# Chunked attention before two feed-forward layers: a block's scores taken one group earlier, beside the transposes of the block before it

## The chip, the core and the metric

The kernel runs on one core of a Trainium2 chip. The metric is the device time of one execution in microseconds (us). Five engines of the core matter here: TensorE (PE in the profile, with its weight loads as PEld), VectorE (DVE), ScalarE (ACT), GpSimd (POOL), and SyncE (SP), which issues the transfers. Each engine takes its instructions in the order in which the program lists them; when the instruction at the head waits, everything behind it on that engine waits too.

## What is computed

Attention over chunks of 64 positions feeds a layer with a cosine gate, and that feeds a second layer without one (4608 tokens, width 512, hidden sizes 2048 and 1024; all in float32):

```python
scores = scale * np.matmul(q_c, k_c.transpose(0, 1, 2, 4, 3))
scores = scores - np.max(scores, axis=-1, keepdims=True)
attn = np.exp(scores)
attn = attn / (np.sum(attn, axis=-1, keepdims=True) + 1e-09)
out = np.matmul(attn, v_c)
...
h = x @ w_in
g = h * np.cos(h)
x = g @ w_out
...
a = x @ w1
b = x @ w2
h = a * b @ w3
return h @ w_out
```

## The kernel before

The 4608 tokens are 9 tiles of 512, numbered 0 to 8. Attention works on 36 blocks of 128 tokens, four to a tile. Every float32 product of the layers is made of three matmuls (lines L107 to L109) on operands that are split into a high and a low half.

The first pass runs over the tiles, and in each tile over five groups of 256 hidden columns of the first layer. While tile n is multiplied, the four blocks of tile n+1 go through attention: block j in one of the first four groups. The fifth group, the end group, has no block; there the finished tile n+1 (`xf`) is split into the seven operands `X` of the next tile (`x_op`, L103: high half on ACT, low half on DVE). Tiles 2 to 7 are of this form. In tile 8 no block is left. A second pass and the second layer follow; there is no attention in them.

What stands where on each engine is written out by hand, as a string with one letter for each step. For the groups of tiles 2 to 8 these are `ORDER1` and, for the end group, `ORDER1E`:

- `1`, `2`, `5`, `3`: the hidden product by seven half-size products of six matmuls each (one in `1`, two in each other step). The results go to PSUM tiles `ps_hh`, which share two banks (pool `ps_h`). DVE adds them: `2` ends with the add `d` (L509), `5` with `e` (L519) and `d` (L521), `3` with `e` (L528). Step `3` needs the bank that the add `d` of step `2` frees.
- `a` `c`, `A` `C`, `b` `d`, `B` `D`: the cosine gate on the halves `d` and `e`: L567 on ACT, L572 on DVE, the cosine L577 on ACT, the product L581 on DVE.
- `s`: the gated group of the step before is split, high half on ACT (L589), low half on POOL (L590), two of each. `x` and `y`: the two halves of the output product of that group, 12 matmuls each into four accumulators `acc`.
- `l`, `m`, `h`, `r`: one weight of a later stage is rebuilt from bit halves (L254 and L289 on ACT; L264 to L267 and L295 on DVE) and written to DRAM. For every second `w_in` weight, `m` also forms sums (L281 to L284). `M`, `H`, `R`: such sums for the weights of groups 0 to 4, the last two of them in tile 2.
- `q`: the next step of the block's attention, in the order scores (L377 on PE; then on DVE the maximum, L386, and the subtraction, L388), exponential (L394 on ACT), sum, reciprocal and scaling (L399 to L402 on DVE, L403 on POOL), transposes (L410 on PE, L413 on ACT), values (L424 on PE, L429 on ACT). Scores, transposes and values share the two banks of the pool `ps_at`.

In an order string the five `q` of a group thus stand for a whole block: the scores behind step `2`, exponential and scaling behind step `5`, the transposes behind `x`, the values behind `y`.

Of the kernel before, what the change touches and what calls it, by code (L numbers as in the profile page):

```python
# [9 lines left out]
F32 = mybir.dt.float32  # L10
# [7 lines left out]
P = 128  # L18
# [3 lines left out]
NJ = NT // P  # L22
HP = 4
CC = 4
G1 = 8
GA = 5
# [11 lines left out]
ORDER0 = "PsvaAqQvqcCqxybBdvDqvq"  # L38
ORDER0E = "PsvaAQvcCxybBodDoooL"
ORDER1P = "PsqMhQqqHaclAxqbCrRmBdyqDL"  # L40
ORDER1PE = "SPsQacATCoobBoxodoDyoo"
ORDER1 = "1s2qMh5qqHa3clAxqbCrRmBdyqDL"
ORDER1E = "S1s25a3cATCoobBoxodoDyoo"
ORDER2 = "1s2h5a3clAxbCrdByDm"
ORDER3 = "12sqhlrmq5a3cAbCdBDxy"
ORDER3B = "12sqhrq5a3clAbCmdBDxy"
# [11 lines left out]
def chunk_attention_two_ffn(  # L58
# [20 lines left out]
    ps_h = ctx.enter_context(tc.tile_pool(name="ps_h", bufs=2, space=bass.MemoryType.PSUM))  # L79
    ps_at = ctx.enter_context(tc.tile_pool(name="ps_at", bufs=2, space=bass.MemoryType.PSUM))  # L80
# [128 lines left out]
    def sum_load(g):  # L209
        pair = ("in", g)  # L210
        loaded.append((g, pair, new_w((pair, 2))))
        nc.sync.dma_start(out=f32(W[pair, 2]), in_=wr[g])
# [35 lines left out]
    def st_low():  # L248

        if sat[1] < sat[0]:  # L250
            now["low"] = key = sq[sat[1]]
            sat[1] += 1
            lo = raws[key][:, :, 0]
            nc.scalar.activation(lo.bitcast(I32), lo, AF.Copy, scale=2.0 ** -29)  # L254
# [32 lines left out]
    def st_hi():  # L287
        for _, x, hi, lo in now.get("parts", ()):
            nc.scalar.activation(hi.bitcast(F32R), x, AF.Copy)  # L289
# [72 lines left out]

    def banks_of(j, early, name):
        return [(ps_acc.tile([P, HP, P], F32, tag=f"acc{2 * (j % 2) + c}", name=f"{name}{c}") if early and name == "ps_s"
                 else ps_h.tile([P, HP, P], F32, tag="h", name=f"{name}{c}") if early
                 else ps_at.tile([P, HP, P], F32, tag="at", name=f"{name}{c}"))[:, 0:2].rearrange("p a (b k) -> p (a b) k", k=64)
                for c in range(2)]
# [35 lines left out]

    def att_transpose(j, early):
        ex = att[j]
        ps = ps_at.tile([P, 512], F32, tag="at", name="ps_at")
        for h in range(HP):
            nc.tensor.transpose(ps[:, P * h:P * h + P], ex[:, 2 * h:2 * h + 2].rearrange("p e k -> p (e k)"), ident)  # L410
        pt = (ex.rearrange("p (h c) k -> p h (c k)", c=2) if early
              else wk.tile([P, HP, P], F32, tag="ex", name="pt"))
        nc.scalar.activation(pt, ps.rearrange("p (h t) -> p h t", h=HP), AF.Copy)  # L413
        att[j] = pt
# [18 lines left out]
    def att_tok(step, early):  # L433
        (att_scores, att_softmax, att_scale, att_transpose, att_values)["ABECD".index(step[0])](int(step[1:]), early)
# [144 lines left out]
    def chain_g(i, h, which):  # L579
        t = rr[i, which]  # L580
        nc.vector.tensor_tensor(out=t, in0=t, in1=h, op=ALU.mult)  # L581

    def split_g(i):

        gg[i] = t = one.tile([P, 8, 256], F32R, tag="g", name="g")
        for which in range(2):
            r = rr.pop((i, which)).rearrange("p (i t) -> p i t", i=2)
            hi, lo = (t[:, 2 * s + which:2 * s + which + (6, 4)[which]:(5, 3)[which]] for s in range(2))
            nc.scalar.activation(hi, r, AF.Copy)  # L589
            nc.gpsimd.tensor_tensor(out=lo, in0=r, in1=f32(hi), op=ALU.subtract)  # L590
# [184 lines left out]
    with tc.manual_schedule():  # L775
# [22 lines left out]
        def order_of(i, nth, end):  # L798
            if i < GA:
                return ORDER0E if end else ORDER0  # L800
            if i < 2 * GA:
                return ORDER1PE if end else ORDER1P
            if i <= iA:
                return ORDER1E if end else ORDER1
            if i < iB:
                return ORDER2
            return (ORDER3X if nxt in xs else ORDER3E) if end else ORDER3B if nth else ORDER3
# [3 lines left out]
        iA, iB = (NTILE - 1) * GA, NTILE * GA  # L811
        n_sums = 0
        fq = 0
        for i in range(NG):
            if i == GA:
                sq.extend(("wo2", j) for j in range(FB2))
# [15 lines left out]
            ps, n, g = groups[i]  # L832
            k_tile = (i - iB) // (G1 - GA)
            nxt = PASS2[k_tile + 1] if 0 <= k_tile < NTILE - 1 else None
            nth = (g, g - GA)[ps]
# [14 lines left out]
            for op in order_of(i, nth, end):  # L850
                if op == "s" and i:
                    split_g(i - 1)
                elif op == "x" and i:
                    x2_mm(i - 1, 0)
                elif op == "y" and i:
                    x2_mm(i - 1, 1)
                elif op == "v":
                    conv_tick()
                elif op == "L":
                    if n_sums < GA:  # L860
                        sum_load(n_sums)
                        n_sums += 1
                elif op == "M":
                    if loaded and i > GA + loaded[0][0]:
                        sum_make()
                elif op in "HR":
                    if sp:
                        {"H": sum_hi, "R": sum_lo}[op]()
                elif op == "l":
                    st_low()  # L870
                elif op == "m":
                    st_bits()
                elif op == "h":
                    st_hi()
                elif op == "r":
                    st_lo()
                elif op in "1253PQ":
                    getattr(z, "step" + op)()
                elif op in "ac":
                    chain_t(i, z.d if op == "a" else z.e, "ac".index(op))  # L880
                elif op in "AC":
                    chain_r(i, z.d if op == "A" else z.e, "AC".index(op))
                elif op in "bd":
                    chain_cos(i, "bd".index(op))
                elif op in "BD":
                    chain_g(i, z.d if op == "B" else z.e, "BD".index(op))
                elif op == "q":
                    if i < iA and nth < 4:
                        att_tok(steps[20 * n + 5 * nth + n_q], False)
                    elif i >= iB + FOLD and fq < 4 * FB2:  # L890
                        need(("w3", fq // 2), *(("wo2", j) for j in range(FB2)))
                        fold(fq // 4, fq % 4)
                        fq += 1
                        if fq == 4 * FB2:
                            load_wf(0)
                            load_wf(1)
                    n_q += 1
                elif op in "ST":
                    x_sums("ST".index(op))
                elif op == "o":  # L900
                    if i < GA and not n_o:
                        x_plain()
                    x_op((z.done if i < GA or i >= 2 * GA else OPS)[n_o], n + 1 if ps == 0 else None)
                    n_o += 1
# [62 lines left out]
        j = FB2  # L967
# [75 lines left out]
```

## Time and profile before

| | |
|---|---|
| device time, median of 3 runs | 1493.02 us (1492.53 to 1494.84) |
| the profiled execution | 1494.28 us |
| its span, first to last instruction | 1492.5 us |
| PE busy | 1445.1 us, 97% of the span |
| DVE busy | 1095.9 us, 73% |
| ACT busy | 686.9 us, 46% |
| POOL busy | 265.0 us, 18% |
| mean granted clock of TensorE | 0.992 |

The ends of matmuls are modelled in the profile, so matmuls overlap in it and a busy PE is not the same as a PE that loses nothing. What a wait costs is better read from the distance of starts. The shares are means over stages with different limits.

### The profile page before, as it was taken

The numbers are of one execution on the slowest core, as the hardware profiler recorded it, in microseconds if no ns is written. First come the engines' busy times: TensorE is split into PE (matmuls) and PEld (weight loads), VectorE is DVE, ScalarE is ACT, GpSimd is POOL, SyncE is SP. The second block draws the span as 40 slices with busy tenths as digits, with TensorE's granted clock in tenths as the row PEclk, the third lists the DMA queues.
The fourth block names the chain that finished last, engine by engine and source line by source line (L and its number), as shares of the span: only waits on it lengthen the run. The fifth ranks groups of instructions, "written<-read, shape, count | busy, mean of one in ns | idle before, by whom it ended". The sixth has DMA issues, their size and how long they took to land.

```text
span 1492.5 us, 26013 instructions
## 1 busy us (share of the span) xinstructions
PE 1445.1 (97%) x9996; PEld 1247.4 (84%) x9996; DVE 1095.9 (73%) x1844; ACT 686.9 (46%) x1173; POOL 265.0 (18%) x194
## 2 busy tenths in 40 slices
PE   5789999999999999999999999999999999999998
PEld 4678888888888889988888889998888888888886
DVE  7976788899898886777777777686565666656553
ACT  4767677787777774444444444231031122014002
POOL 0222222223232222211122222122000100200000
PEclk8999999999999999999999999999999999999999
DMA  8654556465664718999889683586435443631501
GB/s 270 198 189 150 211 177 221 155 248 197 219 227 129 247 65 309 369 323 321 306 296 343 240 309 139 203 319 247 150 111 202 159 148 120 224 136 70 212 23 57
DMA packets 122812, 307.38 MB, mean 206 GB/s; under 512 B 13632, under 2 KB 25664, under 8 KB 121536
## 3 DMA queue, kind: packets, MB, share of 16 engines
q1 hardware_dynamic: 122688, 305.71, 58.6%
q8 instruction: 79, 1.29, 0.4%
q14 instruction: 45, 0.37, 0.1%
HBM read 210.50 MB, written 95.16 MB: 205 GB/s over the span
## 4 chain that ended last, share of the span: by engine, by line
PE 73%; DVE 13%; DMA 5%; ACT 5%; issue 2%; POOL 1%; SPq 1%; DVEq 0%; ACTq 0%; POOLq 0%
PE acc L107 10%; PE acc L108 10%; PE acc L109 10%; PE ps_hh L107 9%; PE ps_hh L109 9%; PE ps_hh L108 9%; PE ps_aa L107 5%; PE ps_aa L108 5%; PE ps_aa L109 5%; ACT L394 2%; POOL ex L403 1%; DVE ex L388 1%; DVE t L572 1%; DVE sm L399 1%; DMA sd<-raw 1%
## 5 line engine op out<-in xcount | busy, mean ns | idle before, releaser
L590 POOL TENSOR_TENSOR g<-t,g 128x512 fp32r<-128x512 f32 x144 | 199.1, 1404 | 562.7 <-ACT g L589 512.2
L107 PE MATMUL acc<-g,w 128*128 128x512 f32 x576 | 228.0, 396 | 0.0
L108 PE MATMUL acc<-g,w 128*128 128x512 f32 x576 | 225.5, 392 | 0.0
L109 PE MATMUL acc<-g,w 128*128 128x512 f32 x576 | 224.4, 390 | 0.0
L109 PE MATMUL ps_hh<-T,w 128*128 128x256 f32 (+1 forms) x616 | 182.3, 296 | 6.7 <-DVE w L200 6.6
L107 PE MATMUL ps_hh<-T,w 128*128 128x256 f32 (+1 forms) x616 | 185.1, 300 | 0.0
L108 PE MATMUL ps_hh<-T,w 128*128 128x256 f32 (+1 forms) x616 | 181.8, 295 | 0.0
L109 PEld LDWEIGHTS acc<-g,w 128*128 128x128 f32 x576 | 108.3, 188 | 23.4
L109 PEld LDWEIGHTS ps_hh<-T,w 128*128 128x128 f32 x616 | 118.7, 193 | 10.0 <-DVE w L200 7.5
L108 PEld LDWEIGHTS acc<-g,w 128*128 128x128 f32 x576 | 108.7, 189 | 19.7 <-POOL g L590 0.6
L107 PEld LDWEIGHTS acc<-g,w 128*128 128x128 f32 x576 | 108.6, 189 | 19.7
L107 PE MATMUL ps_hh<-B,w 128*128 128x256 f32 (+1 forms) x396 | 120.2, 304 | 4.2 <-DVE t L581 2.9
L107 PEld LDWEIGHTS ps_hh<-T,w 128*128 128x128 f32 x616 | 118.6, 193 | 5.4
L108 PEld LDWEIGHTS ps_hh<-T,w 128*128 128x128 f32 x616 | 118.6, 193 | 3.2
L108 PE MATMUL ps_hh<-B,w 128*128 128x256 f32 (+1 forms) x396 | 116.4, 294 | 0.0
L109 PE MATMUL ps_hh<-B,w 128*128 128x256 f32 (+1 forms) x396 | 116.2, 294 | 0.0
L764 ACT ACTIVATE phl<-e 128x512 fp32r<-128x512 f32 x32 | 20.2, 633 | 201.9 <-DVE e L762 201.9
L107 PE MATMUL acc<-wf,phl 128*128 128x512 f32 x252 | 98.3, 390 | 1.4 <-DVE o L707 1.4
L577 ACT ACTIVATE t<-t,half_pi 128x512 f32<-128x512 f32 x144 | 98.3, 715 | 1.4
L108 PE MATMUL acc<-wf,phl 128*128 128x512 f32 x252 | 98.1, 389 | 0.0
L109 PE MATMUL acc<-wf,phl 128*128 128x512 f32 x252 | 98.0, 389 | 0.0
L567 ACT ACTIVATE t<-d 128x512 int32<-128x512 f32 x62 | 38.9, 627 | 120.6 <-DVE d L521 117.9
(209 smaller groups left out, 3419.7 us busy)
## 6 DMA issues: line engine op xcount, KB each, us to landing
w<-sd SPq DMA_DIRECT2D x159, 512.0 KB, 5.9
sd<-raw SPq DMA_DIRECT2D x104, 256.0 KB, 4.6
s<-sd SPq DMA_DIRECT2D x43, 256.0 KB, 4.5
qk<-in_q_dram SPq DMA_DIRECT2D x36, 256.0 KB, 4.5
qk<-in_k_dram SPq DMA_DIRECT2D x36, 256.0 KB, 4.6
x2a<-x2o SPq DMA_DIRECT2D x36, 256.0 KB, 3.0
x2a<-x2a SPq DMA_DIRECT2D x36, 256.0 KB, 6.4
x2d<-x2a SPq DMA_DIRECT2D x36, 256.0 KB, 3.1
```

The source lines that it names most:

```text
L107: nc.tensor.matmul(ps, a[0], b[0], start=first, stop=False)
L108: nc.tensor.matmul(ps, a[0], b[1], start=False, stop=False)
L109: nc.tensor.matmul(ps, a[1], b[0], start=False, stop=last)
L388: nc.vector.tensor_tensor(out=ex[:, :, c], in0=ps[c], op=ALU.subtract, in1=mx[:, :, c].unsqueeze(2).to_broadcast([P, HP, 64]))
L394: nc.scalar.activation(ex, ex, AF.Exp, scale=SCALE)
L399: nc.vector.reduce_sum(out=sm, in_=ex, axis=AX.X)
L403: (nc.vector if early else nc.gpsimd).tensor_tensor(out=ex, in0=ex, in1=rc.unsqueeze(2).to_broadcast([P, 2 * HP, 64]), op=ALU.mult)
L567: nc.scalar.activation(t.bitcast(I32), h, AF.Copy, scale=INV2PI, bias=0.25)
L572: nc.vector.scalar_tensor_tensor(t, h, INV2PI, t.bitcast(I32), op0=ALU.mult, op1=ALU.subtract)
L577: nc.scalar.activation(t, t, AF.Sin, scale=TWO_PI, bias=half_pi)
L590: nc.gpsimd.tensor_tensor(out=lo, in0=r, in1=f32(hi), op=ALU.subtract)
L764: nc.scalar.activation(t[:, 0], e0, AF.Copy)
```

## The change

From tile 2 on the five steps of a block are no longer counted by `q` but named: `6` scores, `7` exponential, `8` scaling, `9` transposes, `0` values. Each has a block counter of its own that starts at block 12 (`MERGED`). `7`, `8`, `9` and `0` stand where a block's own group has them. `6` takes the scores of the following block, right behind the transposes `9`; in the fourth group of a tile it is left out, and the end group takes it instead, between the output product's halves. So scores, maximum and subtraction of a block run one group ahead of its exponential. The transposes of these blocks now take a bank of `ps_h` in place of one of `ps_at`. The number of instructions of each kind stays as it was.

```diff
-ORDER1PE = "SPsQacATCoobBoxodoDyoo"
-ORDER1 = "1s2qMh5qqHa3clAxqbCrRmBdyqDL"
-ORDER1E = "S1s25a3cATCoobBoxodoDyoo"
+ORDER1PE = "SPsQacATCoobBoxo6doDyoo"
+ORDER1 = "1s27Mh58Ha3clAxb96CrRmBdy0DL"
+ORDER1E = "S1s25a3cATCoobBoxo6doDyoo"
...
+    MERGED = 3 * HP
...
-        ps = ps_at.tile([P, 512], F32, tag="at", name="ps_at")
+        ps = (ps_at.tile([P, 512], F32, tag="at", name="ps_at") if j < MERGED
+              else ps_h.tile([P, 512], F32, tag="h", name="ps_ah"))
...
+        at_block = {c: MERGED for c in "67890"}
...
+                elif op in "67890":
+                    j = at_block[op]
+                    if j < NJ and (op != "6" or nth != 3):
+                        att_tok("ABECD"["67890".index(op)] + str(j), False)
+                        at_block[op] += 1
...
-                    if i < iA and nth < 4:
+                    if i < 2 * GA and nth < 4:
```

On PE the second group of tile 6 had this between the halves of the output product, where `ps_at` takes the transposes and `acc` the output product:

```order
L107 MATMUL acc_5758<-g,w 128x512
L108 MATMUL acc_5758<-g,w 128x512
L109 MATMUL acc_5758<-g,w 128x512
L410 MATMUL ps_at<-ident,ex 128x128 x4
L107 MATMUL acc_5755<-g,w 128x512
```

and now has this, with the 32 small matmuls of the scores (`ps_s`), of which two are shown:

```order
L107 MATMUL acc_5758<-g,w 128x512
L108 MATMUL acc_5758<-g,w 128x512
L109 MATMUL acc_5758<-g,w 128x512
L413 MATMUL ps_ah<-ident,ex 128x128 x4
L379 MATMUL ps_s_5779<-qk 64x64
L379 MATMUL ps_s_5780<-qk 64x64
```

The scores left their place between steps `2` and `5` and follow the transposes without a layer product between them.

On DVE, from the add behind step `2` of the same group on, there stood the scores' maximum and subtraction, then the rest of the hidden product, the block's sum, and both halves of the gate (`t<-d`, `t<-e`):

```order
L509 TENSOR_TENSOR d<-x_5662,ps_hh 128x512
L386 TENSOR_REDUCE mx<-ps_s_5684 128x4
L386 TENSOR_REDUCE mx<-ps_s_5685 128x4
L388 TENSOR_TENSOR ex<-ps_s_5684,mx 128x4x64
L388 TENSOR_TENSOR ex<-ps_s_5685,mx 128x4x64
L519 TENSOR_TENSOR e<-d,ps_hh 128x512
L521 TENSOR_TENSOR d<-e,ps_hh 128x256
L399 TENSOR_REDUCE sm<-ex 128x8
...
L528 TENSOR_TENSOR e<-e,ps_hh 128x512
L572 SCALAR_TENSOR_TENSOR t<-d,t 128x512
L572 SCALAR_TENSOR_TENSOR t<-e,t 128x512
L295 TENSOR_TENSOR raw<-cw,raw 128x512
```

Now they stand between the two halves of the gate:

```order
L512 TENSOR_TENSOR d<-x_5689,ps_hh 128x512
L522 TENSOR_TENSOR e<-d,ps_hh 128x512
L524 TENSOR_TENSOR d<-e,ps_hh 128x256
L401 TENSOR_REDUCE sm<-ex 128x8
...
L531 TENSOR_TENSOR e<-e,ps_hh 128x512
L575 SCALAR_TENSOR_TENSOR t<-d,t 128x512
L388 TENSOR_REDUCE mx<-ps_s_5779 128x4
L388 TENSOR_REDUCE mx<-ps_s_5780 128x4
L390 TENSOR_TENSOR ex<-ps_s_5779,mx 128x4x64
L390 TENSOR_TENSOR ex<-ps_s_5780,mx 128x4x64
L575 SCALAR_TENSOR_TENSOR t<-e,t 128x512
L295 TENSOR_TENSOR raw<-cw,raw 128x512
```

The four instructions of the scores went from before the first `e` to behind `t<-d`, and everything from `t<-e` on now follows an instruction that reads the scores of the same group.

On DVE at the end of tile 5, where the splits of the next tile's operands (`B`, `T`, L103) run on into the first group of tile 6, there stood:

```order
L103 TENSOR_TENSOR T_169<-spare,T_169 128x512
L103 TENSOR_TENSOR T_170<-xf,T_170 128x512
L581 TENSOR_TENSOR t<-t,e 128x512
L103 TENSOR_TENSOR B_171<-xf,B_171 128x512
L103 TENSOR_TENSOR T_172<-xf,T_172 128x512
L509 TENSOR_TENSOR d<-x_5481,ps_hh 128x512
L386 TENSOR_REDUCE mx<-ps_s_5503 128x4
```

and there stands now:

```order
L103 TENSOR_TENSOR T_169<-spare,T_169 128x512
L388 TENSOR_REDUCE mx<-ps_s_5451 128x4
L388 TENSOR_REDUCE mx<-ps_s_5452 128x4
L390 TENSOR_TENSOR ex<-ps_s_5451,mx 128x4x64
L390 TENSOR_TENSOR ex<-ps_s_5452,mx 128x4x64
L103 TENSOR_TENSOR T_170<-xf,T_170 128x512
L584 TENSOR_TENSOR t<-t,e 128x512
L103 TENSOR_TENSOR B_171<-xf,B_171 128x512
L103 TENSOR_TENSOR T_172<-xf,T_172 128x512
L512 TENSOR_TENSOR d<-x_5508,ps_hh 128x512
```

The four instructions went from behind the add `d` of the next tile's first group to ahead of three splits, a gate product and that add.

## Rows read from the trace of the kernel before

**Rows 1.** Tiles 2, 5, 6: length; PE, PEld, DVE, ACT, POOL busy (count); clock; DMA.

```profile
176.13:241.33 65.20, 62.23 (x603) 53.37 (x602) 58.06 (x110) 48.35 (x82) 16.98 (x14) 1.00 0.54 180
365.06:427.13 62.07, 61.53 (x603) 53.31 (x602) 55.39 (x104) 47.34 (x79) 18.10 (x14) 1.00 0.62 209
427.13:488.87 61.74, 61.52 (x603) 53.31 (x602) 52.80 (x98) 46.33 (x77) 18.07 (x14) 1.00 0.58 197
```

**Rows 2.** The same view by groups: tile 6's first, second and end group.

```profile
427.13:439.63 12.50, 12.50 (x135) 10.87 (x133) 12.23 (x24) 9.98 (x16) 4.75 (x3) 1.00 0.93 344
439.63:452.51 12.88, 12.81 (x142) 10.94 (x135) 11.21 (x22) 10.21 (x17) 3.58 (x3) 1.00 0.72 226
478.28:488.87 10.59, 10.59 (x72) 9.64 (x67) 9.26 (x16) 7.20 (x15) 2.59 (x2) 1.00 0.31 115
```

**Rows 3.** PE's waits in tiles 2 to 7: who, total us, times, longest.

```profile
PE ps_at L410 <- POOL ex L403: 3.2, 6, 1.8
```

**Rows 4.** PE in order of time around one block's scores: start us, length us, instruction.

```profile
305.10 0.28 PE L108 MATMUL ps_hh<-T,w 128*128 128x256 f32 x1
305.22 0.28 PE L109 MATMUL ps_hh<-T,w 128*128 128x256 f32 x1
305.43 0.69 PE L377 MATMUL ps_s<-qk 64*64 64x64 f32 x32
306.06 0.39 PE L107 MATMUL ps_hh<-T,w 128*128 128x256 f32 x1
306.28 0.28 PE L108 MATMUL ps_hh<-T,w 128*128 128x256 f32 x1
```

**Rows 5.** PE around the same block's transposes.

```profile
311.56 0.39 PE L109 MATMUL acc<-g,w 128*128 128x512 f32 x1
311.79 0.60 PE L410 MATMUL ps_at<-ident,ex 128*128 128x128 f32 x4
312.14 0.48 PE L107 MATMUL acc<-g,w 128*128 128x512 f32 x1
312.46 0.40 PE L108 MATMUL acc<-g,w 128*128 128x512 f32 x1
```

**Rows 6.** DVE in order of time, end of tile 5 and first group of tile 6.

```profile
421.86 0.69 DVE L528 TENSOR_TENSOR e<-e,ps_hh 128x512 f32<-128x512 f32 x1 [0.29 <-PE ps_hh L109]
...
430.30 0.67 DVE L509 TENSOR_TENSOR d<-x,ps_hh 128x512 f32<-128x512 f32 x1
430.90 0.74 DVE L386 TENSOR_REDUCE mx<-ps_s 128x4 f32<-128x256 f32 x2
...
432.23 0.67 DVE L519 TENSOR_TENSOR e<-d,ps_hh 128x512 f32<-128x512 f32 x1
...
436.05 0.68 DVE L572 SCALAR_TENSOR_TENSOR t<-e,t 128x512 f32<-128x512 f32 x1
...
439.14 0.69 DVE L581 TENSOR_TENSOR t<-t,d 128x512 f32<-128x512 f32 x1
439.74 1.28 DVE L612 COPY x2o<-acc 128x512 f32<-128x512 f32 x2
```

**Rows 7.** Tile 8's first two groups, in the view of rows 1.

```profile
550.61:561.66 11.05, 10.90 (x67) 9.57 (x66) 10.05 (x18) 7.10 (x13) 3.70 (x2) 1.00 0.21 62
561.66:572.16 10.50, 10.50 (x67) 9.54 (x66) 8.44 (x15) 5.11 (x10) 2.56 (x2) 1.00 0.52 190
```

**Rows 8.** DVE, PE and POOL in tile 8's first group, in order of time.

```profile
553.78 0.68 DVE L509 TENSOR_TENSOR d<-x,ps_hh 128x512 f32<-128x512 f32 x1
...
554.51 0.38 PE L107 MATMUL ps_hh<-B,s 128*128 128x256 f32 x1
...
552.56 3.70 POOL L590 TENSOR_TENSOR g<-t,g 128x512 fp32r<-128x512 f32 x2 [7.90 <-ACT g L589]
```

**Rows 9.** DVE forming weight sums (tile 3): first of four, then the instruction behind them.

```profile
266.38 0.43 DVE L281 TENSOR_TENSOR spare<-cw 128x256 f32<-128x256 f32 x1
...
268.10 0.68 DVE L581 TENSOR_TENSOR t<-t,d 128x512 f32<-128x512 f32 x1
```

## The prediction

> **What bounds the kernel now.** I read the busy times by tile first. In tile 6 PE is busy for 61.52 of 61.74 us and DVE for 52.80 [rows 1]: PE bounds the stage, and DVE, at 86%, is close behind. By groups, the tile's first takes 12.50 us, the second 12.88, the end group 10.59 [rows 2]. A later group begins behind the small matmuls of the values; coming back from such matmuls costs 0.10 (0.22 instead of 0.12 between starts, [rows 4]). So 12.88 - 12.50 - 0.10 = 0.28 us of the second group is something else. PE's waits name it: the transposes wait for POOL's scaling. That view counts only 6 of these waits, 3.2 us, the longest 1.8 [rows 3]; the others are too short for it and show only in the length of the groups. In the third and fourth group it is the same, so a steady tile loses 3 x 0.28 = 0.84. Tile 5, which also forms weight sums on DVE, takes 0.33 more than tile 6; tile 2, which forms others ahead of the block's sum, 3.46 more [rows 1].
>
> What else waits is seen where the scores are already gone: tile 8 has no block. Its first group takes 11.05 us, its second 10.50 [rows 7]. The 0.55 between them begins where step 3 waits for the add `d`: that starts at 553.78, ends 0.68 later, and step 3 starts at 554.51 [rows 8]. DVE is late there because of the operands' splits. In tiles 2 to 7 the scores stand between steps 2 and 5 and give DVE 0.82 us more; the same add starts 3.17 after the tile's start there too (430.30 - 427.13), and PE doesn't wait for it.
>
> **What the change takes away.** (1) The waits at the transposes: scores, maximum and subtraction are a group ahead, so only exponential, sum and scaling remain in the group. 0.84 us in each tile, the 0.33 in each of tiles 3 to 5 (tile 5 taken for all three), and some of the 3.46.
>
> (2) Switching on PE. Scores inside the hidden product cost 306.28 - 305.22 - 2 x 0.12 = 0.82 us: 0.09 to enter (0.21 between starts instead of 0.12), 0.63 for themselves, 0.10 to come back [rows 4]. Transposes cost nothing to enter and 0.09 to come back (0.32 instead of 0.23, [rows 5]). Behind the transposes the scores share one way back, so they cost 0.64 plus an entry that no row shows: not below 0, as the transposes have it, and 0.09 at most, as the scores have it now. I take the middle, a saving of 0.13 for each of the three blocks that follow transposes, 0.39 a tile; with the bounds 0.27 to 0.54. The fourth block's scores, in the end group, still pay 0.82.
>
> The Trainium skill, page "TensorE: Matmul & The Clock Gate", section "The mechanism", says that a weight load runs beside earlier matmuls only if it goes to other row groups. The transposes use all rows, so by that rule the entry would stay at 0.09 and the sum would come out 0.7 us higher than mine; the trace has no scores directly behind transposes to try it on.
>
> **What it adds: waits on DVE.** DVE does the same work, but two things move on it.
>
> First, the end group. From 421.86 on DVE doesn't pause until the add `d` at 430.30: 14 instructions in 8.44 us, 0.60 each [rows 6]. Now maximum and subtraction, 432.23 - 430.90 = 1.33 us, stand ahead of three splits and that add. The scores themselves are ready by then, so it is only their work. PE's end group grows by 0.82, so the tile starts 0.82 later and the add comes 1.33 - 0.82 = 0.51 later against it: at 3.68 instead of 3.17. But the 0.82 of cover between steps 2 and 5 is gone, and the group now has the shape of tile 8's first one. Step 3 would be due after 30 matmuls at 0.12, 3.60. Tile 8 lost 0.55 with the add at 3.17; at 3.68 the loss is 0.55 + 0.51 = **1.06 us** in the first group of each tile. Its length becomes 12.50 - 0.13 + 1.06 = 13.43.
>
> Second, in the first three groups DVE now waits in the middle. Without maximum and subtraction `t<-e` could start 436.05 - 430.30 - 1.33 = 4.42 after the add, 8.10 into the first group. But ahead of it DVE now holds the maximum, which needs the scores. The output product starts at 42 x 0.12 + 1.06 = 6.10, its half takes 12 x 0.23 = 2.7, the transposes 0.35 (312.14 - 311.79, [rows 5]), the scores 0.63 and an entry: ready at 9.9. DVE stands idle for 1.8 us, and `t<-e`, the staged weight, both gate products and the copies queue behind it. Then 1.33 for the scores, 3.09 from `t<-e` to the gate product (439.14 - 436.05), 0.60 for that, 1.2 for the two copies, 0.60 for the second gate product [rows 6]: DVE is done at 16.7, which is 3.3 into the second group. Its add `d` ends at 4.0, and step 3, due at 3.70, loses 0.28 and, as in tile 8, 0.05 to get the signal and 0.10 to start again; with a little for the low halves I take **0.5 us**. In the second group the scores are ready at 9.35, there are no copies, and DVE ends 2.0 into the third, before step 2 is through at 2.26: no loss. The third is like that, and the fourth has no scores and lets DVE catch up.
>
> A steady tile: 1.06 + 0.5 - 0.84 - 0.39 = **+0.33 us**.
>
> In tiles 3 to 5 one second group forms weight sums on DVE: four instructions, 268.10 - 266.38 = 1.72 us [rows 9]. Before, they cost the 0.33. Now they come on top of a DVE that ends at 2.0: the third group's add starts at 3.75 and ends at 4.43, so step 3 loses 0.9; the low halves on POOL, which come after the second gate product, hold the output product a few tenths more. In the third group there are two more low halves to write (0.60 and 0.43 by their sizes), so the fourth group's add is at about 3.1 and it loses some 0.5 once more. Together 1.5 to 2.4; I take 2.0, net of the 0.33 **+1.7 us** on top of the steady tile.
>
> In tile 2 the other sums still delay the block's own sum, as before, and DVE is even fuller. Not less than 0 (the transposes wait as long as now), not more than 2 (nothing of the two losses of a steady tile is hidden in those waits): I take **+1**.
>
> The sum: 2 x 0.33 for tiles 6 and 7, 3 x 2.0 for tiles 3 to 5, 1 for tile 2: **+7.7 us**. The profiled execution took 1494.28 and would take 1502.0; it lay 1.26 above the median, so as a median **1500.7 us**. With the bounds of each term (entry 0 to 0.09 in 18 places, 1.5 to 2.4 in three tiles, 0 to 2 in tile 2) the sum is 4.4 to 10.7.
>
> Nothing is due for the bank: the transposes' `ps_h` bank is copied out by ACT during the second half of the output product, long before step 2 of the next group needs it; nor for the transfers: q and k of a block are loaded a group ahead as before.
>
> **Rivals.** *Faster*: DVE's idle time covers it. For it: DVE has 8.9 us free in tile 6. Then only the gains count: 5 x 0.84, 3 x 0.33, tile 2's 4.3 and 18 x 0.13 give 11.8, so 1481.2 us. It decides whether the add `d` of a tile's first group starts before 3.60 - 0.68 = 2.9 into it. Against: it stands at 3.17 already and tile 8 pays for it. 7 in 100.
>
> *No difference*: the first group's loss comes, but DVE catches up within it, sums included, and tile 2 keeps its waits. 6 x (1.06 - 0.84 - 0.39) - 3 x 0.33 = -2, so 1491 us. For it: the second groups now have DVE pauses that may take up more than I count. Against: the 1.8 us pause in the middle can't be used, for the engine works in order. 12 in 100.
>
> *Slower than I say*: POOL's low halves become what the output product waits for. In a tile's first group POOL is busy for 4.75 us and in the second for 3.58, with the same three instructions [rows 2]; in tile 8 two low halves take 3.70 and then 2.56 [rows 7]. They are 1.1 us longer where DVE runs splits and gate products beside them. With DVE later, they meet more of these in the first two groups: up to 0.5 more in each, 6 us in all, 1506 us. 13 in 100.
>
> The Trainium skill, page "SBUF — State Buffer", section "SBUF: two separate sides", gives a rule for it: a DVE instruction with two inputs in SBUF and a GpSimd one exclude each other for their whole length, on one shared port pair. The 3.70 against 2.56 agrees.
>
> **The numbers.** 68 in 100 for the forecast, which with its bounds reaches from 1497 to 1504. The range for 8 in 10 takes in the lower part of the slower rival and the upper part of "no difference": 1495.5 to 1505.5. A measurement of this kernel can tell about 0.2%, 3 us. Faster by more 0.08, within it 0.13, slower 0.79.
>
> **What would show it.** Right: no wait of the transposes for POOL in tiles 3 to 7; DVE idle ahead of the maximum (`mx`) for 1 to 2 us in the first three groups of a tile, waiting for PE; step 3 (`ps_hh`) waiting for DVE's `d` in the first group of each tile by about 0.8 and in the second by 0.3; tiles 3 to 5 around 64 us, tiles 6 and 7 at 62.1. Wrong: if the add `d` starts before 2.9 in the first groups, or DVE's pauses ahead of the maximum are under 0.5, the sum falls; if the output product waits for POOL's low halves by more than 0.3 in the first groups, the third rival holds.

## The result, and the profile after

| | before | changed |
|---|---|---|
| device time, median (six runs each) | 1492.69 us (1488.81 to 1494.84) | 1509.84 us (1507.49 to 1513.17) |
| ratio, 95% interval | | 1.012 (1.0106 to 1.0134) |
| the profiled execution, its span | 1494.28, 1492.5 us | 1507.49, 1505.7 us |
| tile 1 | 68.43 us | 69.30 us |
| tiles 2 to 7 | 374.48 us | 392.51 us |
| from tile 8 on | 941.89 us | 936.68 us |

The changed kernel is 17 us slower. The profiled executions differ by 13.2 only. In tiles 1 to 7 the changed one loses 18.9 (18.03 in tiles 2 to 7 and 0.87 in tile 1's end group, where the first block's scores now stand). From tile 8 on it is 5.2 shorter with the same instructions on PE (x4873 in both). Most of that is scatter and not the change: in the profiled executions of the nine kernels below this stretch takes 937.3 to 938.7 us, also in the one with the order of before, so the 941.89 of before is the odd one. The difference between the medians is the better figure for the whole; 18.9 lies within its interval (15.8 to 20.0 us).

The changed kernel by stretches, in the view of [rows 1, 2]: tiles 2, 5 and 6; then tile 6's first, second, third, fourth and end group.

```profile
176.51:245.06 68.55, 62.51 (x603) 53.33 (x602) 60.22 (x109) 49.31 (x82) 17.52 (x14) 1.00 0.53 171
376.96:442.86 65.90, 62.87 (x603) 53.47 (x602) 56.18 (x104) 47.73 (x79) 18.58 (x14) 1.00 0.58 196
442.86:506.38 63.52, 61.81 (x603) 53.39 (x602) 53.74 (x98) 46.98 (x77) 18.62 (x14) 1.00 0.57 191
442.86:456.41 13.55, 12.93 (x136) 10.94 (x134) 11.57 (x24) 9.88 (x16) 5.21 (x3) 1.00 0.83 304
456.41:470.52 14.11, 13.02 (x140) 10.95 (x135) 12.10 (x22) 9.85 (x16) 3.62 (x3) 1.00 0.63 207
470.52:483.14 12.62, 12.62 (x140) 10.98 (x135) 10.03 (x20) 9.65 (x15) 3.60 (x3) 1.00 0.50 146
483.14:494.94 11.80, 11.80 (x108) 10.40 (x103) 10.44 (x19) 9.54 (x15) 3.60 (x3) 1.00 0.51 160
494.94:506.38 11.44, 11.44 (x104) 10.12 (x99) 9.60 (x17) 8.05 (x16) 2.59 (x2) 1.00 0.33 122
```

In tile 6 PE is busy for 61.81 us, about as before, but the tile takes 63.52 instead of 61.74: PE now stands in front of something. The first group is 1.05 longer than before and the second 1.23; the third is 0.26 shorter, the fourth 1.09 shorter (its scores have gone) and the end group 0.85 longer (they came here). The granted clock is 1.00 in every row, so it has no part in this.

Some of what PE waits for in tiles 2 to 7, and the longest of DVE's waits in tiles 3 to 7 (who, total us, times, longest):

```profile
PE ps_hh L107 <- DVE d L512: 14.0, 15, 2.3
PE ps_ah L413 <- POOL ex L405: 2.7, 2, 1.5
PE acc L108 <- POOL g L593: 1.5, 7, 0.2
DVE mx L388 <- PE ps_s L379: 19.1, 15, 1.7
```

The waits of the transposes [rows 3] are gone from this view but for two, both in tile 2. In their place stands step 3's wait for the add `d`, 15 times, and ahead of it DVE's own wait: 15 times its maximum waits for the scores, once for each of the three groups of five tiles.

DVE in order of time, from tile 6's first group into the second, which begins at 456.41. It answers to [rows 6]; the bracket at the end is the idle time before the instruction and what ended it.

```profile
446.50 0.68 DVE L512 TENSOR_TENSOR d<-x,ps_hh 128x512 f32<-128x512 f32 x1
...
452.94 0.76 DVE L388 TENSOR_REDUCE mx<-ps_s 128x4 f32<-128x256 f32 x2 [1.73 <-PE ps_s L379]
...
457.37 0.69 DVE L584 TENSOR_TENSOR t<-t,d 128x512 f32<-128x512 f32 x1
457.97 1.28 DVE L615 COPY x2o<-acc 128x512 f32<-128x512 f32 x2
459.17 1.52 DVE L584 TENSOR_TENSOR t<-t,e 128x512 f32<-128x512 f32 x1
460.61 0.68 DVE L512 TENSOR_TENSOR d<-x,ps_hh 128x512 f32<-128x512 f32 x1
```

POOL and PE beside the last two of these:

```profile
458.85 1.28 POOL L593 TENSOR_TENSOR g<-t,g 128x512 fp32r<-128x512 f32 x1 [8.19 <-PE ps_hh L109]
461.34 0.38 PE L107 MATMUL ps_hh<-B,s 128*128 128x256 f32 x1 [1.09 <-DVE d L512]
```

Two rows carry the case. The maximum stands idle for 1.73 us with everything else of DVE behind it. And the second gate product (`t<-t,e`) takes 1.52 us where the first, of the same shape, takes 0.69: POOL's low half had started 0.32 ahead of it. The add `d` behind it starts 4.20 into the second group, and step 3 on PE waits. In tiles 2 to 7 this product takes 1.49 to 1.52 in each second group.

The trace of before has one such product already, in tile 2's second group; the rows above don't show it:

```profile
192.48 1.63 DVE L581 TENSOR_TENSOR t<-t,e 128x512 f32<-128x512 f32 x1
192.28 1.28 POOL L590 TENSOR_TENSOR g<-t,g 128x512 fp32r<-128x512 f32 x1 [6.43 <-PE ps_hh L109]
```

POOL had started 0.20 ahead there. Of all such products in the trace of before this is the only long one; the median is 0.68.

PE around the scores' new place, which no row of before showed; it answers to [rows 4, 5]:

```profile
451.43 0.39 PE L109 MATMUL acc<-g,w 128*128 128x512 f32 x1
451.66 0.60 PE L413 MATMUL ps_ah<-ident,ex 128*128 128x128 f32 x4
452.19 0.70 PE L379 MATMUL ps_s<-qk 64*64 64x64 f32 x32
452.81 0.50 PE L107 MATMUL acc<-g,w 128*128 128x512 f32 x1
453.15 0.40 PE L108 MATMUL acc<-g,w 128*128 128x512 f32 x1
```

From the transposes' start to that of the scores it is 0.53 us, where four transposes take 0.35 [rows 5]: to enter costs 0.18. From the transposes' start to the second matmul behind the scores it is 1.49. Before, the transposes and the way back took 0.67 (312.46 - 311.79) and the scores elsewhere 0.82: 1.49 as well. Sharing the way back saved nothing.

### The profile page after: what moved, and what is told of

Read it like the earlier page. It is cut to its first block, busy times and chain, and to the rows that moved or that the text cites. A ratio compares the mean times of both kernels' runs of the same rounds, so it can differ in the third digit from the quotient of the medians.

```text
span 1505.7 us, 26047 instructions
## 1 busy us (share of the span) xinstructions
PE 1448.4 (96%) x9996; PEld 1248.3 (83%) x9996; DVE 1100.9 (73%) x1844; ACT 689.7 (46%) x1173; POOL 268.8 (18%) x194
## 4 chain that ended last, share of the span: by engine, by line
PE 77%; DVE 15%; DMA 2%; ACT 2%; issue 2%; POOL 1%; SPq 0%; DVEq 0%; POOLq 0%; ACTq 0%
PE acc L108 11%; PE acc L107 11%; PE acc L109 10%; PE ps_hh L107 10%; PE ps_hh L109 9%; PE ps_hh L108 9%; PE ps_aa L107 5%; PE ps_aa L108 5%; PE ps_aa L109 5%; DVE t L584 2%; POOL g L593 1%; DVE t L575 1%; PE ps_s L379 1%; DVE T L103 1%; DVE mx L388 1%
## 5 line engine op out<-in xcount | busy, mean ns | idle before, releaser
L593 POOL TENSOR_TENSOR g<-t,g 128x512 fp32r<-128x512 f32 x144 | 202.9, 1428 | 609.2 <-ACT g L592 484.9
L592 ACT ACTIVATE g<-t 128x512 fp32r<-128x512 f32 x144 | 86.6, 629 | 35.6 <-DVE t L584 34.0
```

## The experiments

The theory to be tested: all of the loss is DVE's order. The scores' maximum holds DVE at two places (theory A in the texts below), in the end group (which costs the next first group 1 us) and between the gate's halves (which costs the second group), and the second place is dearer than forecast because the gate product then meets POOL's low half (theory B). The rivals: the transposes' new bank or their place beside the scores on PE (theory C); that the order of the low halves could cure the loss by itself; that scores a group ahead cost something wherever they stand; that the switch on PE matters.

### The DVE part of the scores moved behind the gate

`att_scores` is cut in two: the matmuls (`6`), and maximum with subtraction (`w`), which get a place of their own in the strings. Here `w` stands behind `C` and `r` in the first three groups; in the end group it follows the matmuls as in the changed kernel.

```diff
-ORDER1PE = "SPsQacATCoobBoxo6doDyoo"
-ORDER1 = "1s27Mh58Ha3clAxb96CrRmBdy0DL"
-ORDER1E = "S1s25a3cATCoobBoxo6doDyoo"
+ORDER1PE = "SPsQacATCoobBoxo6wdoDyoo"
+ORDER1 = "1s27Mh58Ha3clAxb96CrwRmBdy0DL"
+ORDER1E = "S1s25a3cATCoobBoxo6wdoDyoo"
...
+        scored[j] = ps
+
+    def att_scores_max(j, early):
+        ps = scored.pop(j)
...
+                elif op == "w":
+                    if scored:
+                        att_scores_max(min(scored), False)
```

> The changed kernel with one thing moved on VectorE: in the first three groups of a tile the scores' maximum and subtraction stand behind both halves of the gate's reduction and the low half of the staged weight, not between the two halves of the gate. TensorE's order stays. Theory A (VectorE, held in order at the scores, is late for its add d, which holds step 3): the pause ahead of the maximum in the first group falls from 1.73 us to about 0.5, the second group loses its 1.3 us and tiles 6 and 7 shrink by about 1.3 us each, tiles 3 to 5 by 1.5 to 2.5: 9 to 12 us in all, near 1499. Theory C (the loss is TensorE's, from scores beside transposes and from the transposes' bank among the hidden product's): no change, 1509.8.

Measured: 1495.02 us (ten runs), 1.0016 of before (1.0005 to 1.0028). Tiles 2 to 7 take 377.39. Tile 6's first and second group:

```profile
431.31:444.88 13.57, 12.95 (x135) 10.93 (x133) 12.64 (x26) 10.17 (x16) 5.20 (x3) 1.00 1.02 369
444.88:457.50 12.62, 12.62 (x141) 10.98 (x134) 11.25 (x22) 9.45 (x15) 3.65 (x3) 1.00 0.66 223
```

DVE in order of time in the first group and at the start of the second:

```profile
441.41 0.76 DVE L398 TENSOR_REDUCE mx<-ps_s 128x4 f32<-128x256 f32 x2 [0.56 <-PE ps_s L385]
...
446.44 0.68 DVE L594 TENSOR_TENSOR t<-t,e 128x512 f32<-128x512 f32 x1
```

The pause falls from 1.73 to 0.56, the gate product takes 0.68, and the whole loss of the second group is gone (12.62, the length of a group without a wait). The first group's is untouched. So they are two losses, and the larger one hangs on the place of four DVE instructions: 15.1 of 18 us with the PE order unchanged (392.51 - 377.39). That is more than the 9 to 12 that were expected of this move.

### Only the end group's DVE part moved

Now `w` stays between the gate's halves, and for the end group's scores it comes in the next group, behind the add `d`.

```diff
-ORDER1 = "1s27Mh58Ha3clAxb96CrRmBdy0DL"
+ORDER1 = "1s2w7Mh58Ha3clAxb96wCrRmBdy0DL"
```

> The changed kernel with one thing moved on VectorE: the maximum and subtraction of the scores taken in the end group stand behind the add d of the next tile's first group, where the kernel before has them. TensorE's order stays. Theory A: the add d of a tile's first group starts about 2.4 us into it and not at 3.6; step 3 no longer waits in the first group (1.0 us a tile, 6 us in all), the second group keeps its wait: near 1504. Theory C: no change, 1509.8.

Measured: 1503.47 us (six runs), 1.0068 of before (1.0043 to 1.0093); tiles 2 to 7 take 387.25. The first two groups of tile 6, which begins at 437.39:

```profile
437.39:449.94 12.55, 12.55 (x135) 10.81 (x134) 11.42 (x24) 9.51 (x16) 3.90 (x3) 1.00 0.89 328
449.94:464.26 14.32, 12.99 (x140) 10.96 (x135) 12.31 (x22) 10.04 (x17) 3.62 (x3) 1.00 0.66 203
```

The add `d` on DVE in its first group:

```profile
439.81 0.69 DVE L522 TENSOR_TENSOR d<-x,ps_hh 128x512 f32<-128x512 f32 x1
```

The add starts 2.42 into the tile instead of 3.64 (446.50 - 442.86), and the first group loses its full 1.00, from 13.55 to 12.55. The second keeps its loss (14.32 against 14.11 in the changed kernel). Together with the run above each loss is tied to its own place.

### Before, with the transposes' bank alone

```diff
-        ps = ps_at.tile([P, 512], F32, tag="at", name="ps_at")
+        ps = (ps_at.tile([P, 512], F32, tag="at", name="ps_at") if j < 3 * HP
+              else ps_h.tile([P, 512], F32, tag="h", name="ps_ah"))
```

> The kernel before with only the transposes' bank changed: from block 12 on they take one of the two banks of the hidden product. Orders as before. Theories A and B: same as before, 1492.7, with no new wait of steps 1, 2, 5 or 3. Theory C: part of the 17 us is here, through step 2 or 5 waiting for ScalarE's copy of the transposes.

Measured: 1491.05 us (ten runs), 0.9992 of before (0.9977 to 1.0007). Tile 6:

```profile
424.38:486.14 61.76, 61.54 (x603) 53.31 (x602) 52.80 (x98) 46.30 (x77) 18.09 (x14) 1.00 0.59 197
```

61.76 against 61.74 [rows 1]. The bank costs nothing in the old order, and no wait for it appears. In the new order it is cleared by the runs below that keep it and lose nothing in tile 6 (61.04 and 60.93).

### The second gate product ahead of the copies

The changed kernel with `D` moved ahead of the second half of the output product, so that DVE's product no longer stands behind the two copies of `x2o`. The maximum stays where it is.

```diff
-ORDER1 = "1s27Mh58Ha3clAxb96CrRmBdy0DL"
+ORDER1 = "1s27Mh58Ha3clAxb96CrRmBdDy0L"
```

> The changed kernel with the second gate product ahead of the second half of the output product in the order, so that on VectorE it comes before the two copies of a finished tile's output; VectorE's total work up to the next add d is the same. Theory B (VectorE's gate product and GpSimd's low half shut each other out: it took 1.52 us instead of 0.68 in the second group because GpSimd had just started): the product falls to 0.68, the add d of the second group starts 0.84 earlier, step 3 waits 0.25 and not 1.09, 5 us less in all, near 1505. Plain theory A without a lock: the add d follows the same sum of work, no change in the second group, 1509.8.

Measured: 1504.11 us (four runs), 1.0077 of before (1.0048 to 1.0105); tiles 2 to 7 take 386.68. Tile 6's second group:

```profile
452.08:465.20 13.12, 12.87 (x141) 11.02 (x134) 11.15 (x22) 9.93 (x16) 3.59 (x3) 1.00 0.74 222
```

DVE and POOL at its start, in order of time:

```profile
453.64 0.69 DVE L584 TENSOR_TENSOR t<-t,e 128x512 f32<-128x512 f32 x1
454.25 1.28 DVE L615 COPY x2o<-acc 128x512 f32<-128x512 f32 x2
455.45 0.68 DVE L512 TENSOR_TENSOR d<-x,ps_hh 128x512 f32<-128x512 f32 x1
454.52 2.54 POOL L593 TENSOR_TENSOR g<-t,g 128x512 fp32r<-128x512 f32 x2 [8.18 <-PE ps_hh L109]
```

The product is through before POOL starts and takes 0.69. The add `d` comes 3.37 into the group instead of 4.20, and the group takes 13.12: 0.50 over the 12.62 without a wait. So 0.99 of the second group's 1.49 is the meeting with POOL, and 0.50 is DVE being late by the pause. Of the 0.99, PE's wait ahead of step 3 is 0.84 (1.09 falls to 0.25); the other 0.15 went at the transposes, which came that much late behind POOL's scaling and no longer do. Over the six tiles the edit gives 5.83 us back.

### The second gate product's part split first

The changed kernel with the order of the two halves of a gated group turned round in the split `s`, from tile 2 on: POOL begins with the part of the second gate product, so it can't start before DVE is through with that.

```diff
-        for which in range(2):
+        for which in ((1, 0) if 2 * GA <= i <= iA else (0, 1)):
```

> The changed kernel with the two parts of the gated group's split in the other order (second gate product's part first) in tiles 2 to 8, so that GpSimd cannot start its low halves before VectorE's second gate product is done. Theory B: in the second groups that product takes 0.68 us and not 1.52, the add d starts 0.84 earlier and step 3 waits 0.25 and not 1.09; but both low halves come after it, and the output product then waits for GpSimd by 1 to 1.8, so the second group is 14.1 or longer and the whole not below 1509. Rival (the 1.52 is a wait for ScalarE's cosine, not for GpSimd): the product stays at 1.5 and step 3 waits 1.1 as now.

Measured: 1518.22 us (one run); tiles 2 to 7 take 399.65. DVE and POOL in order of time in tile 6's second group, which begins at 463.34:

```profile
466.09 0.68 DVE L585 TENSOR_TENSOR t<-t,e 128x512 f32<-128x512 f32 x1
466.69 0.68 DVE L512 TENSOR_TENSOR d<-x,ps_hh 128x512 f32<-128x512 f32 x1
467.57 2.53 POOL L594 TENSOR_TENSOR g<-t,g 128x512 fp32r<-128x512 f32 x2 [9.81 <-ACT g L593]
```

One of PE's waits in tiles 2 to 7:

```profile
PE acc L108 <- POOL g L594: 10.6, 13, 1.0
```

The product takes 0.68 again and the add starts 3.35 into the group, as with the product ahead of the copies: two different edits that keep POOL away from it both restore it. But the low halves now start at 467.57, 4.23 into the group instead of 2.44 (458.85 - 456.41), and the output product waits for them 13 times. That is the wait of the third rival in the prediction, brought about by the edit; in this one run it costs more than the late product did. The diagnosis holds, the cure at that place doesn't.

### Both DVE parts moved

```diff
-ORDER1 = "1s27Mh58Ha3clAxb96CrRmBdy0DL"
+ORDER1 = "1s2w7Mh58Ha3clAxb96CrwRmBdy0DL"
```

> Both moves at once, of the scores' maximum and subtraction on VectorE: behind the gate's reductions and the staged low half in the first three groups of a tile, and behind the next group's add d for the scores of the end group. TensorE's order is that of the changed kernel. Theory A: the two losses are separate and both go: tile 6 is 12.55 + 12.62 + 12.62 + 11.80 + 11.44 = 61.0 us (before 61.7, changed 63.5), the whole about 1491. Rival: with the scores behind the add d again, VectorE ends the first group later, its second gate product meets GpSimd's low half as in the changed kernel, and the second group loses 1.5 again: tile 6 near 62.5, the whole near 1499.

Measured: 1488.49 us (twelve runs), 0.9976 of before (0.9962 to 0.9991). Tiles 2 to 7 take 372.19. Tile 6:

```profile
427.37:488.41 61.04, 61.04 (x604) 53.28 (x603) 52.78 (x98) 46.32 (x77) 17.60 (x14) 1.00 0.59 199
```

PE is busy for all of its 61.04 us, and the tile is 0.70 shorter than before. The PE order is that of the changed kernel: with DVE's four instructions elsewhere the same PE program is 20.3 us shorter in tiles 2 to 7.

The product escapes POOL narrowly here. DVE and POOL at the start of the second group:

```profile
441.77 0.68 DVE L594 TENSOR_TENSOR t<-t,e 128x512 f32<-128x512 f32 x1
441.96 2.89 POOL L603 TENSOR_TENSOR g<-t,g 128x512 fp32r<-128x512 f32 x2 [6.88 <-ACT g L602]
```

This time the product is 0.19 ahead; it keeps its length, and POOL's two low halves take 2.89 instead of the 2.54 of the kernel with the product ahead of the copies. In these rows and those of the changed kernel, the one that starts first isn't held.

### The scores ahead of the transposes

The kernel of the last run, with `6` and `9` exchanged.

```diff
-ORDER1 = "1s2w7Mh58Ha3clAxb96CrwRmBdy0DL"
+ORDER1 = "1s2w7Mh58Ha3clAxb69CrwRmBdy0DL"
```

> As e3_both, but on TensorE the scores stand ahead of the transposes, not behind them. It asks what it costs TensorE to go from transposes into scores: in the changed kernel the four transposes take 0.53 us up to the first score matmul and 0.35 up to a matmul of the output product. Theory: the entry into small matmuls is dearer behind transposes (0.17) than behind the output product (0.09), and the way from scores into transposes costs no more than their usual way back (0.10): 0.1 to 0.2 us less for each of 18 blocks, 2 to 3 us less than e3_both. Rival: each change between small and full matmuls costs the same wherever it stands: same as e3_both within 1 us.

Measured: 1490.77 us (twelve runs), 0.9988 of before (0.9977 to 0.9999); tiles 2 to 7 take 372.48, tile 6 60.82. PE around them:

```profile
451.21 0.39 PE L109 MATMUL acc<-g,w 128*128 128x512 f32 x1
451.53 0.69 PE L385 MATMUL ps_s<-qk 64*64 64x64 f32 x32
452.15 0.66 PE L423 MATMUL ps_ah<-ident,ex 128*128 128x128 f32 x4
452.56 0.48 PE L107 MATMUL acc<-g,w 128*128 128x512 f32 x1
```

This way round entering costs 0.09 (0.32 between starts instead of 0.23), the transposes behind the scores 0.41 instead of 0.35. Groups two and three of tile 6 take 12.55 instead of 12.62. The 0.07 is there, but the time doesn't show it: the medians of this run and the last lie 2.3 us apart the other way, where 2 to 3 us less were expected. Tile 3 took 1.00 more in the profiled execution (62.72 against 61.72), and its trace says why: in its second group POOL's low half started 0.14 ahead of the second gate product (260.03 against 260.17), which took 1.70; in tile 6 the product was 0.11 ahead (445.50 against 445.61) and took 0.68. As a gain this order is inconclusive.

### The weight sums of tile 2 later

The idea was that in tile 2 the sums of `M` delay the block's sum, so that moving `M` behind `5` and `8` would shorten it. `D` goes ahead of `y` as well.

```diff
-ORDER1 = "1s2w7Mh58Ha3clAxb96CrwRmBdy0DL"
+ORDER1 = "1s2w7h58MHa3clAxb96CrwRmBdDy0L"
```

> As e3_both, with two more moves on VectorE: the weight sums of tile 2 stand behind the block's sum and reciprocal, not ahead of step 5's adds, and the second gate product ahead of the copies of a finished tile's output. Theory A: tile 2's loss is VectorE's work ahead of the adds and of the block's sum; it falls from about 66 us to 63 or 64, the other tiles stay as in e3_both: 2 to 3 us less than e3_both. Rival: the sums cost the same wherever they stand, since the add of step 3 is then late: tile 2 stays near 66.

Measured: 1489.17 us (twelve runs), 0.9983 of before (0.9970 to 0.9996). Tile 2:

```profile
176.19:243.47 67.28, 63.43 (x604) 55.04 (x602) 57.77 (x111) 48.65 (x82) 16.98 (x14) 0.97 0.51 174
```

The wait of PE that is new in it:

```profile
PE ps_v L437 <- ACT pt L426: 3.6, 2, 2.1
```

Tile 2 takes 67.28 where the kernel without this edit took 66.21. The transposes no longer wait for POOL, and now the values wait for ACT's copy of them, 3.6 us in two places: the wait moved one step on. The two tiles can't be compared to a tenth, for the granted clock was 0.97 in this one and 1.00 in the other; by these means about 2 us of the 67.28 could be the clock's (an estimate: 0.03 of the length). Even so it would not be the 63 to 64 that was expected, and the whole is not 2 to 3 us shorter (1489.17 against 1488.49). The idea isn't borne out.

### A group ahead, at the old place

Scores a group ahead as in the changed kernel, but standing between steps `2` and `5` on PE and DVE, where before had them. Beside the block three things differ from before: the transposes keep their new bank, their copy gets another buffer, and `r` goes ahead of them.

```diff
-ORDER1PE = "SPsQacATCoobBoxo6doDyoo"
-ORDER1 = "1s27Mh58Ha3clAxb96CrRmBdy0DL"
-ORDER1E = "S1s25a3cATCoobBoxo6doDyoo"
+ORDER1PE = "SPsQacATCoobBoxo6wdoDyoo"
+ORDER1 = "1s26w7Mh58Ha3clAxrb9CRmBdy0DL"
+ORDER1E = "S1s26w5a3cATCoobBoxodoDyoo"
...
-              else wk.tile([P, HP, P], F32, tag="ex", name="pt"))
+              else wk.tile([P, HP, P], F32, tag="ex", name="pt") if j < MERGED else wk.tile([P, HP, P], F32, tag="cw", name="pt", bufs=3))
```

> Scores a group ahead, but at their old place between steps 2 and 5 on both engines, in the end group too; maximum and subtraction right behind the add d. So that three tiles of the block can be live, the transposed scores take a buffer of the staged weights, whose low half is written a little earlier in the order. One part of the change alone: a group ahead, without the place behind the transposes. Theory A: the transposes' wait goes (0.28 in three groups), and no wait of step 3 comes: 12.5 + 2 x 12.6 + 11.8 + 11.4 = 60.9 us for tile 6, the whole 1484 to 1488. Rival C (being a group ahead costs by itself, through buffers or banks that are held longer): tile 6 above 61.7 and the whole not below 1492.

Measured: 1487.22 us (twelve runs), 0.9968 of before (0.9954 to 0.9981): the lowest median of all, and under both kernels of this case, though its interval overlaps that of the run with both parts moved. Tiles 2 to 7 take 370.08. Tile 2 and tile 6:

```profile
177.81:244.01 66.20, 63.07 (x603) 55.18 (x602) 57.87 (x111) 48.29 (x81) 17.79 (x14) 0.97 0.53 180
426.84:487.77 60.93, 60.93 (x603) 53.54 (x602) 52.53 (x98) 46.23 (x77) 18.12 (x14) 1.00 0.59 200
```

The three waits that PE has left in tiles 2 to 7:

```profile
PE ps_s L385 <- DMA qk<-in_k_dram: 1.7, 1, 1.7
PE ps_ah L423 <- POOL ex L415: 1.0, 1, 1.0
PE ps_hh L107 <- ACT x L514: 0.5, 1, 0.5
```

All three lie in tile 2, where the granted clock was 0.97. Tiles 3 to 6 take 60.93 to 60.96, weight sums or not. Tile 6 is 0.81 under before: the 0.84 that the prediction read for the waits, to 0.03. So taking scores a group ahead is worth what it was said to be worth, and costs nothing by itself; and the shared way back gives nothing, for with it (the run with both parts moved) tile 6 takes 61.04.

## Why the prediction was wrong in its size

The direction and the main mechanism were right: DVE works in order, the scores' maximum holds it, and step 3 on PE pays through the add `d`. The forecast was +7.7 us, up to 10.7 with every bound; tiles 2 to 7 with the end group of tile 1 (the forecast gave each tile one end group with scores) show +18.9. (By medians it is 1500.7 against 1509.84.) The 11.2 between them, term by term; where the column doesn't say otherwise, measured is tile 6:

| term | forecast | measured |
|---|---|---|
| waits of the transposes, a tile | -0.84 | -0.81 (scores a group ahead, at the old place) |
| first group of a tile, loss | 1.06 | 1.00 |
| second group, loss | 0.5 | 1.49 (step 3 and its restart 1.35, the transposes 0.15) |
| switching on PE, a tile | -0.39 | about 0 |
| tiles 3 to 5 above tile 6 | 2.0 | 2.31 to 2.55 |
| tile 2 | +1 (0 to 2) | +3.35 |

**The step that failed is the second group's 0.5.** It reckoned the second gate product at 0.60, a spacing from [rows 6]. With the product behind the copies it took 1.52, because POOL's low half had started. Where the product was kept away from POOL, the group lost 0.50: the rest of that working (the pause of 1.8, measured 1.73, and the length of DVE's queue behind it) was sound. The edit that puts the product ahead gives 5.83 us back over six tiles. In tile 2, 1.06 of it, the product was held before the change too (1.63); the other 4.8 are new, a little under half of the miss. That one row of before could have warned: it has the meeting and its price.

The meeting of DVE and POOL was in the prediction, as the third rival, but looked at from one side: POOL's low halves made longer by DVE, and the output product waiting for them. The output product's waits for POOL came to 1.5 us in all, none over 0.2, which is under the 0.3 given for that rival. What happened is the reverse: POOL first, DVE held, and PE waiting for DVE.

The Trainium skill, page "SBUF — State Buffer", section "SBUF: two separate sides", says that a DVE instruction with two inputs in SBUF and a GpSimd one that reads SBUF share a port pair, and that whichever starts first has it for its whole length while the other is blocked. The trace agrees but for a tenth: DVE's product ended 0.56 behind POOL's end (460.69 against 460.13), 0.13 short of one undisturbed product after it; in tile 2 of before it was 0.55 (194.11 against 193.56).

**The switching saving was nothing**, 0.39 a tile or 2.3 us in all. The entry from transposes to scores was taken as 0 to 0.09 and is 0.18. Neither neighbour gave it: transposes are free to enter from a layer product, scores cost 0.09 from one, and scores behind transposes cost twice that. Tile 6 took 1.45 more than forecast: 0.99 is the product, 0.39 this saving, and 0.07 small remainders; the last two make 2.8 us over six tiles.

The Trainium skill, page "TensorE: Matmul & The Clock Gate", section "The mechanism", spoke for an entry that stays at 0.09, since a load hides only beside matmuls of other row groups. It was on the right side of my middle, but 0.09 short too. Nor does the trace bear the rule out between matmuls of all rows: in tile 6's first group weight loads are busy for 10.87 of the 12.50 us in which PE is busy throughout [rows 2], and the transposes' first load starts at 451.43, with the layer matmul ahead of them. The scores' first load starts only with their own first matmul, at 452.19.

**Tiles 3 to 5** stand 2.31 to 2.55 above tile 6 (65.83, 66.07 and 65.90 against 63.52), at and over the upper bound of the forecast's 1.5 to 2.4: in tile 5 the third group loses 1.65 (14.27 against 12.62) where 0.9 and a few tenths were given, and the fourth 0.77 (12.57 against 11.80) where it was 0.5. The place was right, the size too small: 1.24 us. Tiles 3 and 4 also had less to win than tile 5, which was taken for them (61.86 and 61.87 before, not 62.07): 0.41. Together 1.7 us of the miss.

**Tile 2** exceeded its upper bound of 2 by 1.35, and the forecast's middle by 2.35. The two waits of the transposes stayed (2.7 us), and the bound had set a steady tile's two losses beside them at their forecast sizes. The product is no part of this miss, for it was held before as well. With both DVE parts moved tile 2 takes 66.21: 2.34 of its 3.35 hang on the place of the four DVE instructions (0.57, 0.90 and 0.88 in its first three groups). Beyond the 0.46 for switching and remainders, 1.9 us of the miss lie here; how the third group's 0.88 comes about, without a product that is held, stays open.

The sum: 4.8 + 2.8 + 1.7 + 1.9 = 11.2.

The other rivals. *Faster* was decided by an add `d` before 2.9 in the first group; it came at 3.64. With the end group's part moved it comes at 2.42 and that loss vanishes, so the point was well put. *No difference* needed DVE to catch up within the first group; the 1.73 us that it stands in the middle can't be made up, as was argued. Forecast and measured for the first group (1.06 and 1.00) show that the reading from tile 8, which has the group's shape without its scores, carried over. It was put down to step 3 whole, though. In tile 8 step 3 and its restart are 0.41 of the 0.55; the other 0.15 lie at the output product's first matmuls (556.04, 556.31 and 556.65, where 0.23 between starts is usual), as POOL's low halves end at 556.26 [rows 8]. In tile 6 of the changed kernel it is 0.88 and 0.14: the sum came out because both were carried over together.

## What to carry to other kernels

When a step is moved on one engine, its followers on other engines need not move with it: the PE order of this change was sound (20 us shorter in tiles 2 to 7 with four DVE instructions elsewhere), and an instruction that waits belongs where its operand is already there, not where its producer is. When an engine is made late by some amount, look at what its late instructions will then run beside: a price taken from rows where they ran alone doesn't hold there, and a rival that names two engines in contention has to be worked out in both directions. And here the cost of changing from one kind of matmul to another could not be read from the two kinds' costs towards a third.

## What the hardware showed that was not expected

A DVE product of 128x512 with two inputs took 1.52 us instead of 0.69 when a GpSimd subtraction of 1.28 us had started 0.32 before it, and 0.68 and 0.69 in the two kernels that kept them apart. Where the product started 0.11 to 0.19 first, it kept its 0.68, and the two GpSimd subtractions took 2.89 and 2.99 us instead of 2.54. The two copies of `x2o` (from PSUM, 1.28 us for two) kept that length beside GpSimd's 2.54 us for two in the run with the product ahead.

32 score matmuls of 64x64 directly behind four 128x128 transposes start 0.18 us later than the transposes alone account for; behind a layer product it is 0.09, and transposes behind scores lose 0.06.
